# Loading v in f32, updating the state in two operations, and transposing more pairs by the DMA crossbar in a tuned recurrence-plus-MLP kernel

## The chip, the cores and the metric

The kernel runs on one core of one Trainium2 chip. The metric is the device time of one execution in microseconds (us). Each comparison ran on one chip, with runs of the kernel before in between. Every profiled run is of the fast state. Medians are of all runs of a kernel. Ratios leave out the runs classed slow (over 1.5% above the fastest of the same kernel): two of four in the run with a later order, one each in three others, and three of six in one, where it is said.

## The reference

A gated linear recurrence over 768 steps, for 4 batches and 8 heads of 48, feeds an MLP with gelu (384 to 2048 to 384). All inputs and the output are f32.

```python
state = zeros(B, H, D, D)                       # B, H, S, D = 4, 8, 768, 48
for t in range(S):
    state = alpha[:, :, t, :, None] * state + einsum('bhd,bhe->bhde', k[:, :, t], v[:, :, t])
    y[:, :, t] = einsum('bhd,bhde->bhe', q[:, :, t], state)
x = y.transpose(0, 2, 1, 3).reshape(B * S, H * D)
h = x @ w_in                                    # 384 x 2048
out = gelu_tanh(h) @ w_out                      # 2048 x 384
```

## The kernel before

The 768 steps are cut into 6 chunks of 128 tokens, and the 4 batches go in twos: 12 *pairs* (chunk, two batches), numbered 0 to 11. Pair by pair the kernel does this:

- loads a (alpha), q, k, v of the pair from DRAM; GpSimd (POOL) issues these loads for pairs 2 to 11;
- forms the decays (`la` = ln a, a running sum `cum` on TensorE, exps `b`, `binv`, `bend`) on ScalarE (ACT), and the scaled q' (`qp`) and k' (`kp`) on VectorE (DVE);
- transposes q' and k' into `qkT`, multiplies them (`at`), masks the product (`atm`), and forms y (`yps`) from it, v and the state;
- transposes x = y into `xT`, runs layer 1 (`hT`), gelu (`gT`), layer 2 (`acc`), and stores (`ot`).

A transpose is done either by TensorE (a product with an identity matrix, then an eviction from PSUM) or by a DMA through the crossbar, issued by SyncE (SP). Two tuples say which pairs take the DMA. `DECAYS` says in which phase of layer 1 the ln and exps of a pair are done.

```python
DECAYS = {-1: (0, 1), 1: (2, 3), 2: (4,), 3: (5,), 4: (6, 7), 5: (8,), 6: (9,), 7: (10,), 8: (11,)}
TURN_QK, TURN_X = (8, 9, 10, 11), (7, 8, 9, 10, 11)
...
def load(self, n, c, i, lo=0, hi=2):            # n: "a", "q", "k" or "v"
    def emit(e):
        if n not in u:
            u[n] = self.tile(n, [C, 2, H, D], BF16 if n == "v" else F32)
        src = self.src[n][2 * i + lo:2 * i + hi].rearrange("b h s d -> s (b h) d")[c * C:(c + 1) * C]
        (nc.sync if e == "SP" else nc.gpsimd).dma_start(u[n][:, lo:hi].rearrange("t b h d -> t (b h) d"), src)
...
def turn_dma(self, u, n):                       # q' or k' of a pair, both batches
    self.nc.sync.dma_start_transpose(self.qkT(u)[:, "qk".index(n)].rearrange("d i p t -> d (i p) t"),
                                     u[n + "p"].rearrange("t i h d -> t (i h d)"))
def turn_x_dma(self, u, i, c, b):               # x of one batch
    self.nc.sync.dma_start_transpose(self.xT[c][:, :, b, :], u["x", i])
...
def carry(self, u, i, c, b):                    # state update of one batch
    for o in range(2):                          # the two heads of a head pair
        ps, fs = slice(64 * o, 64 * o + 64), slice(D * o, D * o + D)
        acc = kv[ps, :, fs]
        if c > 0:
            nc.vector.tensor_tensor(s[ps], acc, old[ps, :, fs], op=ALU.add)
            acc = s[ps]
        nc.vector.tensor_tensor(new[ps, :, fs], acc, u["bend"][ps, i, :, None].to_broadcast([64, H // 2, D]), op=ALU.mult)
```

Every engine runs its instructions in a fixed order. The program makes it when it is built, by list scheduling over tasks with assumed costs, buffers and landing times. For a transpose by DMA it assumes that the data is there `landed + xbar` after the issue: 2.2 + 1.5 = 3.7 us for q' or k', one after the other, and 3.2 us for x, with 2.5 us more for early pairs (`late`). Where the assumption is too short, an engine stands at an instruction although later ones could run.

```python
landed=2200, xbar_qk=1500, xbar_x=1000, late_x=2500
...
if t.kind in ("turn", "store"):
    xbar = t.done = max(xbar, t.end + W["landed"] - t.xbar) + t.xbar
    t.done += t.late
...
tq = [s.add("turn", {"SP": W["turn"]}, P + 10, self.turn_dma(u, n), d, xbar=W["xbar_qk"])
      for n, d in (("q", qp), ("k", kp))]
```

## Time and profile before

| | before |
|---|---|
| median time | 185.78 us (184.66 to 186.07) |
| span of the profiled run | 183.2 us |
| TensorE busy | 175.7 us, clock granted in full |
| first layer-1 matmul (`hT`) | 17.21 us |

The expectations below say 17.4 us for the first `hT`, as the chain that ended last has its first piece of `hT` at 17.38 us; all starts in this text are from the order on TensorE. TensorE is the bound, as the lines in the prediction show. Two more views also belong here. The first is the table of DMA queues on the page: queue, packets, megabytes, and the time that its packets took as a share of 16 engines. q0 carries the loads that GpSimd issues, q1 what SP issues.

```profile
DMA packets 51206, 27.76 MB, mean 151 GB/s; under 512 B 38833, under 2 KB 48241, under 8 KB 51185
...
q0 software_dynamic: 32096, 17.70, 69.0%
q1 hardware_dynamic: 18512, 9.38, 21.5%
```

Most packets are small. Sorted by size, the trace has 24,576 packets of 96 B (one row of v, cast to bf16 by its load), 2,944 of about 4 KB (f32 loads: 18 to 24 rows of 192 B in a packet, mostly 22) and 12,032 of 256 B (transposes). These counts were there to be read before the prediction, and the prediction does not use them.

The second view is the order on VectorE in the start (start, length, what; in brackets the idle time before it and what ended it):

```profile
11.11 2.48 DVE L431 TENSOR_TENSOR atm<-at,ut 128x512 bf16<-128x512 f32 x4 [0.82 <-PE at L424]
15.38 1.02 DVE L354 TENSOR_TENSOR qp<-q,b 128x384 bf16<-128x384 f32 x2 [1.78 <-ACT x L480]
```

The four masks of pair 0 come first, then the q' of pair 1.

### The profile page before, as it was taken

Reading aid. Unit: us, or ns where it says so; the run is one execution under the profiler, and the core shown is the slowest. Engines: PE = TensorE matmul, PEld = TensorE weight load, DVE = VectorE, ACT = ScalarE, POOL = GpSimd, SP = SyncE. Lnnn points to the kernel's source line nnn. Section 1 sums busy time; section 2 is a strip of 40 time slices with the busy share of each in tenths; the row PEclk is TensorE's granted clock in tenths of the full one; section 3 lists DMA queues with packets and bytes.
Section 4 is the critical chain, followed back from the end, with each engine's and each line's share of the span. In section 5 each row is a group of like instructions: output and inputs, shape, how many; then the busy total and the mean of one; then the engine's idle time right before and its main releaser. Section 6 shows DMA issues by size and latency. Waiting matters only on the chain.

```text
span 183.2 us, 4630 instructions
## 1 busy us (share of the span) xinstructions
PE 175.7 (96%) x1861; PEld 129.3 (71%) x1861; DVE 104.2 (57%) x232; ACT 135.6 (74%) x310; POOL 60.9 (33%) x68
## 2 busy tenths in 40 slices
PE   7887999999999999999999999999999999999993
PEld 2465869666686787687688769678677677686873
DVE  7775954065969896597499798298644715000000
ACT  3666969873888789859799768899789884491941
POOL 2595837975545755564750200000000000000000
PEclk9999999999999999999999999999999999999999
DMA  5999999999999999999999955753271290311102
GB/s 155 187 242 211 187 231 214 204 202 174 195 281 183 169 229 197 181 225 205 180 213 235 179 171 100 104 115 67 52 170 46 43 202 4 88 43 47 43 0 86
DMA packets 51206, 27.76 MB, mean 151 GB/s; under 512 B 38833, under 2 KB 48241, under 8 KB 51185
## 3 DMA queue, kind: packets, MB, share of 16 engines
q0 software_dynamic: 32096, 17.70, 69.0%
q1 hardware_dynamic: 18512, 9.38, 21.5%
q10 hardware_dynamic: 576, 0.39, 0.7%
q8 instruction: 14, 0.23, 0.6%
q14 instruction: 8, 0.06, 0.1%
HBM read 25.17 MB, written 4.72 MB: 163 GB/s over the span
## 4 chain that ended last, share of the span: by engine, by line
PE 85%; DMA 6%; ACT 3%; DVE 2%; SPq 1%; ACTq 1%; issue 0%
PE acc L516 34%; PE hT L497 31%; PE at L424 4%; PE qkT_ps L364 4%; PE yps L473 3%; DMA a<-in_alpha_dram 2%; PE yps L470 2%; DMA q<-in_q_dram 2%; PE cum L320 2%; PE kv L441 2%; DMA qkT<-kp 2%; PE xT_ps L487 1%; DVE atm L431 1%; ACT L503 1%; PE cum L322 1%; SPq L247 1%
## 5 line engine op out<-in xcount | busy, mean ns | idle before, releaser
L497 PE MATMUL hT<-xT,w_in 128*128 128x256 bf16 x576 | 70.1, 273 | 0.4 <-ACT gT L503 0.4
L503 ACT ACTIVATE gT<-hT 128x256 bf16<-128x256 f32 x192 | 63.4, 387 | 8.6 <-PE hT L497 8.3
L516 PE MATMUL acc<-w_out,gT 128*128 128x384 bf16 (+1 forms) x400 | 68.8, 319 | 0.0
L497 PEld LDWEIGHTS <-w_in 128*128 128x128 bf16 x576 | 54.0, 98 | 8.0 <-issue 0.6
L516 PEld LDWEIGHTS <-gT 128*128 128x128 bf16 x400 | 36.8, 98 | 19.6
L431 DVE TENSOR_TENSOR atm<-at,ut 128x512 bf16<-128x512 f32 x48 | 30.9, 685 | 15.0 <-PE at L424 14.5
L354 DVE TENSOR_TENSOR qp<-q,b 128x768 bf16<-128x768 f32 (+1 forms) x15 | 11.7, 794 | 18.7 <-ACT b L343 15.8
L528 ACT COPY ot<-acc 128x384 f32<-128x384 f32 (+1 forms) x18 | 8.3, 462 | 13.9 <-PE acc L516 12.6
L235 POOL DMA_DIRECT2D v<-in_v_dram x13 | 14.6, 1123 | 9.6 <-PE hT L497 2.9
L235 POOL DMA_DIRECT2D k<-in_k_dram x11 | 12.2, 1112 | 11.0 <-DVE kp L354 5.2
L343 ACT ACTIVATE b<-cum 128x768 bf16<-128x768 f32 (+1 forms) x15 | 10.2, 684 | 6.7 <-PE cum L322 3.1
L235 POOL DMA_DIRECT2D q<-in_q_dram x11 | 12.3, 1114 | 7.0 <-DMA k<-in_k_dram 1.8
L235 POOL DMA_DIRECT2D a<-in_alpha_dram x11 | 12.3, 1114 | 5.9 <-ACT gT L503 2.2
L213 ACT ACT_TABLE_LOAD x9 | 11.5, 1283 | 2.8 <-issue 2.6
L480 ACT CAST x<-yps 128x384 bf16<-128x384 f32 x16 | 7.7, 481 | 7.8 <-PE yps L473 7.6
L458 DVE TENSOR_TENSOR st<-stmp,bend 64x192 bf16<-64x192 f32 x32 | 11.3, 353 | 1.5
L354 DVE TENSOR_TENSOR kp<-k,binv 128x768 bf16<-128x768 f32 (+1 forms) x15 | 11.8, 792 | 0.2
L456 DVE TENSOR_TENSOR stmp<-kv,st 64x192 f32<-64x192 f32 x32 | 11.3, 352 | 1.0 <-PE kv L441 0.7
L503 ACT ACT_TABLE_LOAD x9 | 11.5, 1283 | 0.2
L222 PE MATMUL idle<-zero 128*128 128x512 bf16 x27 | 9.5, 462 | 1.2 <-DVE blk L778 1.2
L382 DVE COPY qkT<-qkT_ps 128x1024 bf16<-128x1024 bf16 (+1 forms) x13 | 8.7, 688 | 3.0 <-PE qkT_ps L364 2.9
L343 ACT ACTIVATE binv<-cum 128x768 bf16<-128x768 f32 (+1 forms) x15 | 10.1, 683 | 0.0
(62 smaller groups left out, 159.4 us busy)
## 6 DMA issues: line engine op xcount, KB each, us to landing
out_dram<-ot SPq DMA_DIRECT2D x23, 192.0 KB, 2.3
a<-in_alpha_dram POOLq DMA_DIRECT2D x9, 384.0 KB, 13.1
q<-in_q_dram POOLq DMA_DIRECT2D x9, 384.0 KB, 13.2
k<-in_k_dram POOLq DMA_DIRECT2D x9, 384.0 KB, 13.3
v<-in_v_dram POOLq DMA_DIRECT2D x11, 192.0 KB, 13.3
w_in<-in_moe_w_in_dram POOLq DMA_DIRECT2D x4, 384.0 KB, 7.7
w_out<-in_moe_w_out_dram POOLq DMA_DIRECT2D x4, 384.0 KB, 9.8
a<-in_alpha_dram SPq DMA_DIRECT2D x6, 96.0 KB, 3.4
```

The lines of the kernel that those rows point to most:

```text
L213: nc.scalar.add_instruction(mybir.InstLoadActFuncSet(name=nc.get_next_instruction_name(), act_func_set_id=i, engine=mybir.EngineType.Activ ...
L222: self.nc.tensor.matmul(ps, self.zero[:, 0:self.C], self.zero, start=True, stop=True)
L235: (nc.sync if e == "SP" else nc.gpsimd).dma_start(u[n][:, lo:hi].rearrange("t b h d -> t (b h) d"), src)
L343: self.nc.scalar.activation(u[n].rearrange("t i h d -> t i (h d)")[:, lo:hi], cum, AF.Exp, scale=1.0 if n == "b" else -1.0)
L354: self.nc.vector.tensor_tensor(out, rows, b, op=ALU.mult)
L382: self.copy(e)(t, ps)
L431: self.nc.vector.tensor_tensor(u["atm", i][:, o], u["at", i][o], self.ut[:, None, :].to_broadcast([self.C, self.H // 2, self.C]), op=ALU.mult)
L456: nc.vector.tensor_tensor(s[ps], acc, old[ps, :, fs], op=ALU.add)
L458: nc.vector.tensor_tensor(new[ps, :, fs], acc, u["bend"][ps, i, :, None].to_broadcast([64, H // 2, D]), op=ALU.mult)
L497: self.nc.tensor.matmul(h, self.w_in[:, j, nt * self.C:(nt + 1) * self.C], self.xT[c][:, j, lo:hi].rearrange("p g t -> p (g t)"), start=j ...
L503: return lambda e: self.nc.scalar.activation(self.gT[c % self.NG][:, nt, lo * self.C:hi * self.C], f.pop(("h", c, lo, nt)), AF.Gelu_apprx_ ...
L516: self.nc.tensor.matmul(f["acc", c, b][:, lo:hi], self.gT[c % self.NG][:, nt, b * self.C:(b + 1) * self.C], self.w_out[:, nt, lo:hi], star ...
```

## The change

Four things change together; letters are used below.

- **A**: v arrives in f32 by plain loads and is narrowed to bf16 on chip, by VectorE for pairs 0 and 1 and by GpSimd for the others.
- **B**: the state update covers both heads of a head pair in one add and one multiply of 128x384, with decays `ends` that are zero off the diagonal blocks.
- **C**: q', k' of pairs 5, 6, 7 and x of pairs 5 and 6 are transposed by DMA as well, so that TensorE does less.
- **D**: the decays of pair 5 move to the phase of pair 4's, and pair 6's one phase ahead.

```diff
-    DECAYS = {-1: (0, 1), 1: (2, 3), 2: (4,), 3: (5,), 4: (6, 7), 5: (8,), 6: (9,), 7: (10,), 8: (11,)}
+    DECAYS = {-1: (0, 1), 1: (2, 3), 2: (4, 5), 3: (6,), 4: (7,), 5: (8,), 6: (9,), 7: (10,), 8: (11,)}
-    TURN_QK, TURN_X = (8, 9, 10, 11), (7, 8, 9, 10, 11)
+    TURN_QK, TURN_X = (5, 6, 7, 8, 9, 10, 11), (5, 6, 7, 8, 9, 10, 11)
-    BUFS = dict(..., ot=6, bend=8, a=4, q=4, k=4, v=6)
+    BUFS = dict(..., ot=5, bend=3, ends=8, a=4, q=4, k=4, v=3, vb=4)
...
-                u[n] = self.tile(n, [C, 2, H, D], BF16 if n == "v" else F32)
+                u[n] = self.tile(n, [C, 2, H, D], F32)
+    def narrow(self, u, lo, hi):
+        (self.nc.gpsimd.tensor_copy if e == "POOL" else self.nc.vector.tensor_copy)(u["vb"][...], u["v"][...])
+    def ends(self, u):
+        nc.vector.tensor_tensor(ends, bend broadcast, self.half broadcast, op=ALU.mult)     # 16 elements
...
-            for o in range(2):
-                ... two operations of 64x192 each
+            nc.vector.tensor_tensor(s, acc, old, op=ALU.add)
+            nc.vector.tensor_tensor(new..., acc..., ends, op=ALU.mult)
```

The diff is shortened; `...` marks what is left out. The assumed costs of v's loads in the start (`early_0`, `early_1`, `share`) and of the state operations change with it. The assumed landing of a transpose does not.

More of the change, by code (lines that the diff above doesn't have):

```diff
@@ L17 @@
     cum=530, cum_packed=1500, t8=450, t4=225, attn=340, kv=170, inter=170, intra=205, tx=168, l1_4=655, l1_2=340, l2=655,
-    qk2=910, qk1=500, ev8=650, ev4=350, mask=640, st=1400, st0=700, xc=520, xe=330, ot=540,
+    qk2=910, qk1=500, ev8=650, ev4=350, mask=640, st=1090, st0=545, end=110, xc=520, xe=330, ot=540,
     ev8_act=960, ev4_act=520, xc_act=450, xe_act=450, ot_act=450,
-    strip=2120, cast=1500, weight=2080, dma=2100, issue=1100, wissue=760, sp=100, store=2600, turn=1250, landed=2200, xbar_qk=1500, xbar_x=1000, late_x=2500, piece=330, late_k=1500, piece_issue=450, begin=2700, cast_0=1300, share=1200, cast_1=1900, ln_packed=1040, cold=380, fill=216, zero=1100,
+    strip=2120, weight=2080, dma=2100, issue=1100, wissue=760, sp=100, store=2600, turn=1250, landed=2200, xbar_qk=1500, xbar_x=1000, late_x=2500, piece=330, late_k=1500, piece_issue=450, begin=2700, early_0=1000, share=1000, early_1=1400, vb1=300, vb2=550, vb1_pool=600, vb2_pool=950, ln_packed=1040, cold=380, fill=216, zero=1100,
 )
@@ L156 @@
     URGENT = (2,)
-    BUFS = dict(ca=1, yk=2, ff=4, la=3, qp=4, kp=4, b8=2, kn=2, qkT=4, atm=6, x=3, ot=6, bend=8,
-                a=4, q=4, k=4, v=6)
+    BUFS = dict(ca=1, yk=2, ff=4, la=3, qp=4, kp=4, b8=2, kn=2, qkT=4, atm=6, x=3, ot=5, bend=3, ends=8,
+                a=4, q=4, k=4, v=3, vb=4)
     def __init__(self, ctx, tc, q, k, v, alpha, w_in, w_out, out):
@@ L182, in __init__ @@
         self.ident = const.tile([C, C], BF16, name="ident")
+        self.half = const.tile([C, 2], F32, name="half")
         self.ones = const.tile([C, 1], F16, name="ones")
@@ L345, in exp, with emit @@
         return emit
+    def narrow(self, u, lo, hi):
+        def emit(e):
+            if "vb" not in u:
+                u["vb"] = self.tile("vb", [self.C, 2, self.H, self.D], BF16)
+            (self.nc.gpsimd.tensor_copy if e == "POOL" else self.nc.vector.tensor_copy)(u["vb"][:, lo:hi].rearrange("t b h d -> t (b h d)"), u["v"][:, lo:hi].rearrange("t b h d -> t (b h d)"))
+        return emit
     def scaled(self, u, n, lo, hi):
@@ L441, in emit @@
                 nc.tensor.matmul(kv[:, p, :], u["kn" if u["packed"] else "kp"][:, i, 2 * p:2 * p + 2, :].rearrange("t h d -> t (h d)"),
-                                 u["v"][:, i, 2 * p:2 * p + 2, :].rearrange("t h d -> t (h d)"),
+                                 u["vb"][:, i, 2 * p:2 * p + 2, :].rearrange("t h d -> t (h d)"),
                                  start=True, stop=True)
+        return emit
+    def ends(self, u):
+        C, H = self.C, self.H
+        def emit(e):
+            t = u["ends"] = self.tile("ends", [C, 2, H // 2, 2], F32)
+            (self.nc.gpsimd if e == "POOL" else self.nc.vector).tensor_tensor(
+                t.rearrange("f i p o -> f (i p) o"), u["bend"].rearrange("f i p -> f (i p)")[:, :, None].to_broadcast([C, H, 2]),
+                self.half[:, None, :].to_broadcast([C, H, 2]), op=ALU.mult)
         return emit
@@ L449, in emit @@
         def emit(e):
-            kv, old, new = u["kv", i], self.state[b][c % 2], self.state[b][(c + 1) % 2]
-            for o in range(2):
-                ps, fs = slice(64 * o, 64 * o + 64), slice(D * o, D * o + D)
-                acc = kv[ps, :, fs]
-                if c > 0:
-                    s = self.sb.tile([C, H // 2, D], F32, tag=f"stmp{o}", bufs=2, name="stmp")
-                    nc.vector.tensor_tensor(s[ps], acc, old[ps, :, fs], op=ALU.add)
-                    acc = s[ps]
-                nc.vector.tensor_tensor(new[ps, :, fs], acc,
-                                        u["bend"][ps, i, :, None].to_broadcast([64, H // 2, D]), op=ALU.mult)
+            acc, old, new = u["kv", i], self.state[b][c % 2], self.state[b][(c + 1) % 2]
+            if c > 0:
+                s = self.sb.tile([C, H // 2, 2 * D], F32, tag="stmp", bufs=2, name="stmp")
+                nc.vector.tensor_tensor(s, acc, old, op=ALU.add)
+                acc = s
+            ends = u["ends"][:, i].rearrange("f p o -> f (p o)")[:, :, None].to_broadcast([C, H, D])
+            nc.vector.tensor_tensor(new.rearrange("f p (o d) -> f (p o) d", o=2),
+                                    acc.rearrange("f p (o d) -> f (p o) d", o=2), ends, op=ALU.mult)
         return emit
@@ L472, in emit @@
             for h in range(H):
-                nc.tensor.matmul(y[:, h, :], u["atm", i][:, h % 2, h // 2, :], u["v"][:, i, h, :],
+                nc.tensor.matmul(y[:, h, :], u["atm", i][:, h % 2, h // 2, :], u["vb"][:, i, h, :],
                                  start=c == 0, stop=True, skip_group_check=True)
@@ L548, in load @@
             nonlocal n
-            land = W[{"v": "cast", "w": "weight"}.get(key[0], "strip")]
-            loads[key] = s.add("load", {"POOL": cost}, n, emit, gate, land=W[f"cast_{key[1]}"] if key[0] == "v" and key[1] in self.PACKED else land * 3 // 8 if key[0] != "w" and key[1] in self.SPLIT else land,
+            land = W[{"w": "weight"}.get(key[0], "strip")]
+            loads[key] = s.add("load", {"POOL": cost}, n, emit, gate, land=W[f"early_{key[1]}"] if key[0] == "v" and key[1] in self.PACKED else land * 3 // 8 if key[0] != "w" and key[1] in self.SPLIT else land,
                                late=W["share"] if key[:2] == ("v", 0) else 0)
@@ L599, in tasks @@
             early = m in self.EARLY
-            lns[m], ends[m], qp, kp, be = [], [], [None, None], [None, None], [None, None]
+            lns[m], ends[m], qp, kp, be = [], [], [None, None], [None, None], []
             cums, exps = [], []
@@ L611, in tasks @@
                 if u["sums"]:
-                    be[lo:hi] = [x[2]] * n
+                    be.append(x[2])
                 ends[m].append(x[-1])
@@ L644, in tasks @@
                 owner = every[0]
+            if u["sums"]:
+                end = s.add("end", {"DVE": W["end"]}, P + 16, self.ends(u), be)
+            narrow = [None, None]
+            for lo, hi in ((0, 1), (1, 2)) if early else self.parts(m):
+                n = hi - lo
+                narrow[lo:hi] = [s.add("vb", {"DVE": W[f"vb{n}"]} if early else {"POOL": W[f"vb{n}_pool"]}, P + 9 if early else -1, self.narrow(u, lo, hi),
+                                       [loads["v", m, lo]])] * n
+            loads["v", m, 0].take("v", *narrow)
             for j in range(2):
@@ L670, in tasks @@
                 y = s.add("y", {"PE": W["intra"] + (W["inter"] if c else 0)}, P + 20 + j, self.y(u, j, c, b),
-                          ms + turned + [loads["v", m, j]] + ([states[b, c - 1]] if c else []))
+                          ms + turned + [narrow[j]] + ([states[b, c - 1]] if c else []))
                 xc = s.add("x", {"ACT": W["xc_act"], "DVE": W["xc"]}, P + 20 + j, self.x(u, j), [y])
@@ L692, in tasks @@
                         backs.append(tb)
-                    kv = s.add("kv", {"PE": W["kv"]}, P + 30 + j, self.kv(u, j), [k, loads["v", m, j]])
+                    kv = s.add("kv", {"PE": W["kv"]}, P + 30 + j, self.kv(u, j), [k, narrow[j]])
                     st = states[b, c] = s.add("st", {"DVE": W["st" if c else "st0"]}, P + 30 + j, self.carry(u, j, c, b),
-                                              [kv, be[j]] + ([states[b, c - 1], ys[b, c - 1]] if c else []))
+                                              [kv, end] + ([states[b, c - 1], ys[b, c - 1]] if c else []))
                     kv.take("yk", st)
@@ L710, in tasks @@
             kp[0].take("kp", *tq, *kvs)
-            loads["v", m, 0].take("v", *vs)
+            narrow[0].take("vb", *vs)
             if u["sums"]:
-                be[0].take("bend", *cs)
+                be[0].take("bend", end)
+                end.take("ends", *cs)
         n = 0
@@ L778, in run @@
         nc.vector.memset(self.blk, 0.0)
+        nc.vector.memset(self.half, 0.0)
+        for o in range(2):
+            nc.vector.memset(self.half[64 * o:64 * o + 64, o:o + 1], 1.0)
         for t in self.ut_blk:
```

## The prediction

> **What bounds the kernel now.** I read the busy table and the slices first. TensorE (PE) is busy 96% of the span and its clock is granted in full in every slice, so PE is the candidate; a mean hides stages, so I asked for the busy time by stretch next.
>
> ```profile
> PE 175.7 (96%) x1861; PEld 129.3 (71%) x1861; DVE 104.2 (57%) x232; ACT 135.6 (74%) x310; POOL 60.9 (33%) x68
> ...
> PE   7887999999999999999999999999999999999993
> ...
> DMA  5999999999999999999999955753271290311102
> ```
>
> ```profile
> 17.00:28.50 11.50, 11.24 (x142) 8.84 (x140) 8.00 (x17) 9.10 (x24) 7.59 (x10) 1.00 1.46 206
> 28.50:180.30 151.80, 151.20 (x1601) 113.01 (x1598) 84.28 (x165) 117.14 (x266) 43.59 (x39) 1.00 0.88 144
> ```
>
> The second fence has two stretches: length, then busy PE, weight loads, DVE, ACT, POOL. From 28.5 to 180.3 us PE idles 151.80 - 151.20 = 0.6 us. Before that lie a start bounded by loads and by short DVE and ACT steps, and after it a tail of 2.9 us of eviction and store. "Busy" could be padding, so I checked the pace in the chain that ended last: 48 matmuls of hT in 5.24 us are 109 ns each, and 16 of acc in 2.60 us are 163 ns each, without holes. So the middle is a full PE pipe: a matmul taken away there is time taken away, as long as nothing new makes PE wait. The other row that matters is DMA: full until slice 23 (some 107 us) and mostly idle afterwards.
>
> These lines of the chain (start, length, what) are the PE work that the change moves off PE:
>
> ```profile
> 77.44 0.89 PE qkT_ps L364 x16
> ...
> 86.67 0.17 PE xT_ps L487 x3
> ...
> 91.80 0.89 PE qkT_ps L364 x16
> ```
>
> Sixteen transposes turn q' and k' of one pair of batches, in 0.89 us (55.6 ns each); three turn x of one batch, in 0.17 us.
>
> [...] The trace has 352 and 353 ns for the two state operations and 552 to 555 ns for 128x384 products[...]. [...] an output store, also issued by SP, takes 7.7 us to land beside the loads and 2.1 us after them. [...]
>
> **The change, part by part.**
>
> *Transposes by DMA for more pairs.* q' and k' of pairs 5, 6, 7 leave PE: 3 x 16 x 55.6 ns = 2.67 us. x of pairs 5 and 6 leaves PE: 2 pairs x 2 batches x 3 x 55.6 ns = 0.67 us. All of it lies in the stretch from 77 to 107 us, where PE never idles: **3.34 us off the path**. The evictions go from DVE too: 6 of qkT at 687 ns and 4 of xT at 352 ns, 5.5 us, beside PE work and worth nothing by themselves. In their place come 6 transposes of q', k' and 4 of x on the SP queue. What they take when the queue is quiet, and what the load beside them does, is here (first row from 30 to 108 us, the others from 108 to 160 us; the last number is us from issue to landing):
>
> ```profile
> out_dram<-ot SPq DMA_DIRECT2D x11, 192.0 KB, 7.7
> ```
>
> ```profile
> out_dram<-ot SPq DMA_DIRECT2D x9, 192.0 KB, 2.1
> xT<-x SPq DMA_TRANSPOSE x10, 2.3
> qkT<-qp SPq DMA_TRANSPOSE x4, 3.2
> qkT<-kp SPq DMA_TRANSPOSE x4, 3.1
> ```
>
> All eight transposes of q', k' and all ten of x now run after the loads. The new ones run among them. If they lose what a store loses (7.7 - 2.1 = 5.6 us), q' and k' land some 9 us after issue and x some 8 us: an estimate from these rows.
>
> *Decays one phase ahead.* This is to pay for that latency. Pair 5's ln and exps move from ACT's turn at 71 to 77 us to the one at 56 to 64 us, beside pair 4's; pair 6's from the turn at 85 to that at 71. The count of turns stays nine, so table loads stay 18 x 1.28 us. A turn with two pairs is longer: the present one runs 85.27 to 94.05 us, 8.8 us, against 71.12 to 77.41, 6.3 us, for one pair. PE lost nothing at the present double turn (10.00 of 10.00 us busy from 80 to 90 and from 90 to 100), since it has 5.2 us of acc and the pair's attention to do; the new double turn also still has pair 4's transposes on PE. So I count 0. Inputs: a of pair 5 was issued at 42.55 us and lands some 13.1 us later, at 55.7; its q and k at about 58 and 59.4, just in time for products at 61 to 64.
>
> Timing for pair 5: transposes issued at about 64 to 66 us, landed at 67 to 69 (quiet) or 73 to 75 (loaded). The present at of pair 5 starts at 78.99, so data that late still meets the present position. x: even if its y stays at 82.5 and 85.5 us, x is issued by about 86.5 and lands by 94.5 loaded, against hT of pair 5 at about 91.8; but attention that is ready earlier is placed earlier, as with pairs 8 to 11 now, and then x has over 8 us.
>
> *v in f32.* [...] POOL issues at the pace of landings from 55 to 95 us;[...] steps are 1.5 to 1.9 us for a v load and 1.7 to 2.2 us for an f32 one. Some 0.35 us more for ten loads is 3.5 us of DMA time, all before 108 us and off the path. Narrowing on POOL: nine of 128x768 and two halves[...]. On DVE: four narrowings of 128x384 for pairs 0 and 1, at most 0.56 us each, in the start. No transpose now runs while a casting load is in flight (the last v lands at about 99 us, the first transpose is at 110.04), and I take it that v goes to f32 to let transposes in earlier.
>
> *State update.* Now:
>
> ```profile
> L458 DVE TENSOR_TENSOR st<-stmp,bend 64x192 bf16<-64x192 f32 x32 | 11.3, 353 | 1.5
> L456 DVE TENSOR_TENSOR stmp<-kv,st 64x192 f32<-64x192 f32 x32 | 11.3, 352 | 1.0 <-PE kv L441 0.7
> ...
> L458 DVE TENSOR_TENSOR st<-kv,bend 64x192 bf16<-64x192 f32 x8 | 2.8, 355 | 0.8 <-ACT gT L503 0.7
> ```
>
> 25.4 us in all. [...] DVE is 57% busy and PE waits for it only in the start, so I count 0 in the middle.
>
> **The sum.** 3.34 us off PE. In the start, narrowing v of pairs 0 and 1 on DVE can put 0.2 to 0.5 us ahead of the first hT, and the shorter first state updates give back some; I count a loss of 0.3 us. 185.8 - 3.3 + 0.3 = **182.8 us**, 1.6% less.
>
> **The rivals.** (a) *A new wait of PE for a transpose under load.* For: PE executes in a fixed order made with an assumed landing of 3.7 us for q', k' (2.2 + 1.5 in the kernel's own table) and nothing for load, where stores lose 5.6 us; if at is placed as soon as the order thinks it ready, PE stands for the difference. x has 2.5 us of allowance. Against: at also waits for one shared PSUM buffer, and hT can run first. One stall of 2 to 5 us would give 185 to 188 us; small ones 183 to 184. (b) *DMA or POOL becomes the bound:* POOL waits for v to land before it can narrow, holds back later loads, and ACT's new double turn starts late for want of a, q, k of pair 5, which have 1 to 2 us in hand. It would give 183.5 to 185. Against: about six loads stand in the queue, 13 us of work. (c) *More than PE's share:* the start is gated by DVE steps of 0.3 to 0.7 us and contains fills of PE; if f32 v lands sooner and DVE is freer, 0.5 to 1.5 us more, 181 to 182. (d) *ACT becomes the bound* as PE's phases shorten to about 12.5 us: against it, the present phase without PE transposes, 128.40 to 140.78 us, shows PE full and ACT below 80%.
>
> **Range and chances.** The gain of PE work is nearly certain, its keeping is not. Half of (c) gives 181, a moderate (a) or (b) 185.5: range 181.0 to 185.5. Faster by over 2% means below 182.06, which needs about 0.4 us of (c) beyond the pure PE gain: 0.31. Slower by over 2% needs stalls of 7 us in all: 0.05. Within 2%: 0.64.
>
> **What would show it.** PE transposes fall by 48 and 12, to 80 of q', k' (of 128) and 30 of x (of 42). In the middle PE idles under 1 us; if (a) holds, waits of PE or its weight loads for DMA qkT or DMA xT appear at 65 to 108 us. [...] The first hT stays within 0.5 us of 17.2 us. DMA stays full some 4 to 8 us longer. The prediction is wrong if transposes under load take over 10 us, or if the start moves by over 1 us.

## The result, and the profile after

| | before, same rounds | after |
|---|---|---|
| median time | 185.22 us (184.31 to 186.07) | 224.12 us (223.19 to 224.63) |
| ratio | | 1.209 (95%: 1.202 to 1.217) |
| span of the profiled run | 183.2 us | 222.2 us |
| TensorE busy | 175.7 us | 180.0 us |

Ratios here are the mean time of one kernel's fast runs over the mean of the other's fast runs of the same rounds, so they are not quite the ratio of the medians. The kernel is 21% slower, far outside the range.

The busy table and the slices of the kernel after (40 slices of 5.6 us; PE and DMA in tenths busy, PEclk the granted clock in tenths):

```profile
PE 180.0 (81%) x1804; PEld 129.4 (58%) x1804; DVE 100.4 (45%) x209; ACT 134.0 (60%) x304; POOL 69.3 (31%) x79
...
PE   7859999999999104991089806989999999999993
...
PEclk9999999999999755999559975899999999999999
DMA  5999999999999995199913993160341706130102
```

TensorE has three deep holes, and after each its clock is at about half (a 5 in the slices above). The waits say at what it stands (engine, line, what ended the wait: total us, times, longest):

```profile
PEld L432 <- DMA qkT<-kp: 34.5, 5, 13.7
PE at L432 <- DMA qkT<-kp: 33.2, 4, 13.4
POOL a L236 <- ACT x L496: 17.8, 2, 17.3
...
POOL vb L352 <- PE yps L489: 14.6, 1, 14.6
```

The chain that ended last holds the same three transposes, of pairs 5, 6 and 7 (start, length, what), 44 us in all:

```profile
19.57 0.49 PE hT L513 x3
...
68.73 17.54 DMA qkT<-kp
...
97.32 14.60 DMA qkT<-kp
...
123.49 11.83 DMA qkT<-kp
```

The landings, from the view of DMA issues cut at 60, 80, 110 and 140 us, one pair in each (the last number is us from issue to landing; the same transposes took 3.2 and 3.1 us before):

```profile
qkT<-qp SPq DMA_TRANSPOSE x1, 18.7
qkT<-kp SPq DMA_TRANSPOSE x1, 17.5
...
qkT<-qp SPq DMA_TRANSPOSE x1, 6.6
qkT<-kp SPq DMA_TRANSPOSE x1, 14.6
...
qkT<-qp SPq DMA_TRANSPOSE x1, 10.9
qkT<-kp SPq DMA_TRANSPOSE x1, 11.8
```

**Where the 39.0 us went.** TensorE's idle time grew from 183.2 - 175.7 = 7.5 us to 222.2 - 180.0 = 42.2 us, that is by 34.7 us; 33.2 us of it is the wait of `at` for k'. Its busy time grew by 4.3 us although 60 transposes left it. The work removed was 3.3 us, so the rest runs 7.6 us longer. Some 1.0 us of that is three more padding matmuls; the remaining 6.6 us fits the half clock after the holes (for example 0.50 granted from 86 to 88 us, 0.72 from 88 to 90, 1.00 from 90 on). The trace's record of the clock has it at half until 89.1, 116.4 and 140.3 us, that is over 2.8, 4.5 and 4.9 us of work after the three holes; half of these 12.2 us is 6.1 us. The holes are of 13.4, 11.0 and 8.5 us, and the record has half clock from 75.45, 106.17 and 130.07 us, that is from 2.6, 5.2 and 3.2 us into them. Shorter holes in the experiments below went both ways. One of 2.3 us (43.3 to 45.6 us) in the first run of "One pair less" was followed by half clock from 46.6 to 53.5 us, and three of 0.7 to 0.94 us between 92.3 and 95.8 us in the run with small packets on the kernel before by half clock from 95.2 to 98.6 us. One of 2.9 us in the run with small packets and a later order was not. What length of hole brings the half clock is not shown by these runs.

**Why the transposes were late.** The records of the DMA packets were counted by queue and size. Rates are packets per us of each of the 16 engines:

| stretch | f32 load packets (4 KB, about 290 ns each) | transpose packets (256 B, about 30 ns each beside loads, 18 ns without) |
|---|---|---|
| after, 74 to 78 us | 3.2 | 3.7 |
| after, 78 to 82 us | 3.2 | 4.8 |
| after, 82 to 86.5 us | 1.2 | 19.3 |
| after, 172 to 180 us, no loads | 0 | 19.0 |

The first row can be read, near enough, from the view of DMA queues for 74 to 78 us (queue: packets of all 16 engines, megabytes, share; 34 of the packets of q0 are not of a load but of 4 B):

```profile
q0 software_dynamic: 237, 0.83, 94.0%
q1 hardware_dynamic: 236, 0.06, 11.4%
```

While both queues have work, one transpose packet goes through for about each load packet: 3.7 and 4.8 beside 3.2 in the first two rows. I read this as each engine taking the two queues in turn, a packet from each. That is my estimate from the near equality of the two columns; the order in which an engine takes packets was not looked at. A load packet of 290 ns and a transpose packet of 30 ns, one after the other, would let about 3.1 of each through per us. Where few loads are queued, the counts part: from 98 to 102 us, POOL having just issued again, 19.4 transpose packets passed beside 1.9 load packets.

q' of a pair is 1,024 packets, and k' another 1,024: 128 per engine. At 3.7 per us they need 35 us. They did not need that long because the stall itself ended it: with TensorE at `at`, buffers were not freed, POOL stood (17.8 and 14.6 us above, and 17.3 us more in a line left out), no new loads were issued, the queue ran dry between 82 and 84 us and the transposes then went at 19 per us.

### The profile page after: what moved, and what is told of

Its sections match the earlier page's. It is cut to its first block, busy times and chain, and to the rows that moved or that the text cites. A ratio compares the mean times of both kernels' runs of the same rounds, so it can differ in the third digit from the quotient of the medians.

```text
span 222.2 us, 4524 instructions
## 1 busy us (share of the span) xinstructions
PE 180.0 (81%) x1804; PEld 129.4 (58%) x1804; DVE 100.4 (45%) x209; ACT 134.0 (60%) x304; POOL 69.3 (31%) x79
## 4 chain that ended last, share of the span: by engine, by line
PE 62%; DMA 25%; DVE 3%; ACT 3%; issue 2%; SPq 2%; POOL 0%; DVEq 0%; ACTq 0%
PE acc L532 26%; PE hT L513 22%; DMA qkT<-kp 21%; PE at L432 3%; DMA q<-in_q_dram 3%; PE yps L489 2%; SPq L248 2%; PE yps L486 2%; PE qkT_ps L372 1%; PE cum L321 1%; DMA a<-in_alpha_dram 1%; ACT L519 1%; PE xT_ps L503 1%; PE idle L223 1%; PE kv L449 1%
## 5 line engine op out<-in xcount | busy, mean ns | idle before, releaser
L519 ACT ACTIVATE gT<-hT 128x256 bf16<-128x256 f32 x192 | 64.1, 386 | 45.7 <-PE hT L513 45.1
L513 PE MATMUL hT<-xT,w_in 128*128 128x256 bf16 x576 | 72.8, 281 | 1.1 <-ACT gT L519 1.1
L513 PEld LDWEIGHTS <-w_in 128*128 128x128 bf16 x576 | 56.0, 100 | 11.1 <-issue 2.5
L432 PE MATMUL at<-qkT 64*128 64x128 bf16 x192 | 10.2, 233 | 33.2 <-DMA qkT<-kp 33.2
L432 PEld LDWEIGHTS <-qkT 64*128 64x128 bf16 x192 | 5.9, 99 | 39.2 <-DMA qkT<-kp 34.5
L236 POOL DMA_DIRECT2D a<-in_alpha_dram x11 | 12.2, 1108 | 38.1 <-ACT x L496 17.8
L362 DVE TENSOR_TENSOR qp<-q,b 128x768 bf16<-128x768 f32 (+1 forms) x15 | 11.8, 793 | 14.3 <-ACT b L344 11.9
L236 POOL DMA_DIRECT2D q<-in_q_dram x11 | 12.2, 1106 | 6.5 <-DVE qp L362 3.3
L236 POOL DMA_DIRECT2D k<-in_k_dram x11 | 12.2, 1107 | 3.5 <-DMA w_out<-in_moe_w_out_dram 1.2
L352 POOL CAST vb<-v 128x768 bf16<-128x768 f32 (+1 forms) x11 | 8.5, 783 | 14.6 <-PE yps L489 14.6
L362 DVE TENSOR_TENSOR kp<-k,binv 128x768 bf16<-128x768 f32 (+1 forms) x15 | 11.8, 792 | 0.1
L223 PE MATMUL idle<-zero 128*128 128x512 bf16 x30 | 10.5, 454 | 1.2 <-DVE half L804 1.2
L474 DVE TENSOR_TENSOR st<-stmp,ends 128x384 bf16<-128x384 f32 x16 | 10.6, 664 | 0.5
L496 ACT CAST x<-yps 128x384 bf16<-128x384 f32 x11 | 5.3, 478 | 8.1 <-PE yps L489 7.7
## 6 DMA issues: line engine op xcount, KB each, us to landing
a<-in_alpha_dram POOLq DMA_DIRECT2D x9, 384.0 KB, 12.2
q<-in_q_dram POOLq DMA_DIRECT2D x9, 384.0 KB, 12.5
```

Of the source, the lines that this page charges most:

```text
L223: self.nc.tensor.matmul(ps, self.zero[:, 0:self.C], self.zero, start=True, stop=True)
L352: (self.nc.gpsimd.tensor_copy if e == "POOL" else self.nc.vector.tensor_copy)(u["vb"][:, lo:hi].rearrange("t b h d -> t (b h d)"), u["v"][ ...
L362: self.nc.vector.tensor_tensor(out, rows, b, op=ALU.mult)
L432: nc.tensor.matmul(at[o][:, p, :], t[sl, 1, p, :], t[sl, 0, p, :], start=True, stop=True)
L474: nc.vector.tensor_tensor(new.rearrange("f p (o d) -> f (p o) d", o=2), acc.rearrange("f p (o d) -> f (p o) d", o=2), ends, op=ALU.mult)
L513: self.nc.tensor.matmul(h, self.w_in[:, j, nt * self.C:(nt + 1) * self.C], self.xT[c][:, j, lo:hi].rearrange("p g t -> p (g t)"), start=j ...
```

## The experiments

Fourteen kernels were run; all gave correct results. Twelve came before and two after the last open question was stated.

### Undo C alone

```diff
-    TURN_QK, TURN_X = (5, 6, 7, 8, 9, 10, 11), (5, 6, 7, 8, 9, 10, 11)
+    TURN_QK, TURN_X = (8, 9, 10, 11), (7, 8, 9, 10, 11)       # from the kernel after
```

> The changed kernel with q', k' of pairs 5 to 7 and x of pairs 5, 6 turned on TensorE again; f32 v, narrowing, two-operation state and earlier decays stay. Theory (T): the loss is TensorE standing before the late q', k' transposes, 33 us of waits and some 5 us of slow clock after them; without them 185 to 189 us, and no wait of TensorE over 2 us after 30 us. Rival (R1): f32 v, the narrowing on POOL or the earlier decays hold up the inputs and the transposes are only where it shows; then above 200 us.

Measured: 188.26 us against 185.68, ratio 1.017 (1.010 to 1.025). Nothing waits for `qkT`, and TensorE waits 2.2 us at most for any one thing. So C with its waits is some 36 of the 39 us; A, B and D keep a loss of some 2.6 us. The loss is in the start: the first `hT` is at 20.91 us instead of 17.21. DMA is full only to slice 19 of 40 here, against slice 23 before, so loading v in f32 did not lengthen that stretch; that it shortened it is not shown, since with B alone and v still cast (below) DMA is full to slice 18.

### C and D alone, on the kernel before

```diff
-    DECAYS ... 2: (4,), 3: (5,), 4: (6, 7) ...     # from the kernel before
+    DECAYS ... 2: (4, 5), 3: (6,), 4: (7,) ...
-    TURN_QK, TURN_X = (8, 9, 10, 11), (7, 8, 9, 10, 11)
+    TURN_QK, TURN_X = (5, 6, 7, 8, 9, 10, 11), (5, 6, 7, 8, 9, 10, 11)
```

> The kernel before with only the transposes and the earlier decays of the change; v cast by the DMA, four-operation state. T: loads stand in the queue as before, so the waits of at for qkT come here too: 205 to 230 us. R1, or that plain f32 v loads are what delays the transposes (R3): under 195 us.

Measured: 223.44 us, ratio 1.210 (1.198 to 1.222). The wait:

```profile
PE at L424 <- DMA qkT<-kp: 36.4, 4, 20.8
```

The stall is there in full with v cast by its load and the old state update. A and B neither cause it nor cure it. The first `hT` is at 17.36 us, so C and D do not move the start. Part of this stall is of another kind than the one worked out above; see what stays open.

### Tell the order that q', k' land late

```diff
-  self.turn_dma(u, n), d, xbar=W["xbar_qk"])
+  self.turn_dma(u, n), d, xbar=W["xbar_qk"], late=14000 * (m < 8))   # from the kernel after
```

> The changed kernel, with 14 us added to the landing that the order assumes for q', k' of pairs 0 to 7, so that TensorE gets at of these pairs later. T: the transposes still take over 10 us to land beside the loads, but TensorE has other work in front of them: waits for qkT fall from 33 us to under 6, 184 to 191 us. If the transposes cost more than a badly placed wait (they hold up the loads, R4), above 200 us.

Measured: 221.53 us, ratio 1.186 (1.170 to 1.201); the expectation was missed. TensorE went on past the old place, so loads went on too, and q', k' of pair 5 took longer than before:

```profile
qkT<-qp SPq DMA_TRANSPOSE x1, 26.0
qkT<-kp SPq DMA_TRANSPOSE x1, 30.6
...
PE at L432 <- DMA qkT<-kp: 13.6, 2, 12.4
...
PE hT L513 <- DMA xT<-x: 8.7, 1, 8.7
```

The number came out where the expectation had put its rival. From 74 to 91 us, 3.0 load packets and 3.5 transpose packets passed per us and engine: the shares of the kernel after, for 17 us on end. From 91 to 101 us the loads thinned out as well (1.6 per us), so the 30.6 us stay somewhat under the 35 us worked out above. This separates two readings: it was not only an order that knew too little, the transposes lacked throughput beside the loads. A phase takes some 12.5 us, and in it q', k' and the x of two batches need 128 + 48 packets per engine, which at 3 to 4 per us is over 40 us.

### Smaller load packets

```diff
-                u[n] = self.tile(n, [C, 2, H, D], F32)      # from the kernel after
+                u[n] = self.tile(n, [C, 2, H, D], F32 if u["m"] < 3 else F16 if n == "a" else BF16)
```

The loads of pairs 3 to 11 cast, so they move in packets of 96 B, one row each. It rounds the inputs earlier and is not meant as a version to keep.

> The changed kernel, with a (to f16), q, k and v (to bf16) of pairs 3 to 11 cast by the DMA: the same number of 192-byte rows, but I expect one small packet per row instead of packets of 4 KB. T in the form that transposes share the DMA engines packet by packet with the loads (T-packet): q', k' of pairs 5 to 7 land in 3 to 7 us and the time is 182 to 190 us. Rival (R2): the DMA engines are full and a transpose waits for its share of bytes or behind what is queued, whatever the packets: 11 to 19 us to land, over 205 us. The result may be off by more than the reference allows, since a, q, k are rounded earlier.

Measured: 207.27 us, ratio 1.120 (1.110 to 1.130). q' and k' land in 7.3 to 9.0 us. From 71 to 75 us, where both queues have work throughout, the view of DMA queues has:

```profile
q1 hardware_dynamic: 1736, 0.44, 83.4%
q0 software_dynamic: 1854, 0.18, 80.9%
```

That is 27 and 29 packets per us and engine: about one for one again, with some nine times as many load packets as above (29 against 3.2), each of 28 ns instead of 290. The packet size is the cause, then: the order is the same and the bytes read are the same. (The edit also halves the bytes that these loads write. The DMA engines were full in these 4 us all the same; a run with fewer bytes in packets of 4 KB was not made.) The landing stays above the assumed 3.7 us, so TensorE still stands:

```profile
PE at L432 <- DMA qkT<-kp: 16.2, 4, 6.1
```

### Smaller packets and an order that knows

```diff
+  late=7000 * (m < 8)                              # on top of the run with smaller load packets
```

> The run with a, q, k, v cast by the DMA from pair 3 on (one 96-byte packet per row), with 7 us added to the landing that the order assumes for q', k' up to pair 7. Theory: with small packets in the other queue the crossbar has the throughput, 7 to 9 us a pair, so once the order knows it TensorE need not stand: waits for qkT fall from 16 us to under 4, 184 to 190 us. Rival: with the loads going on (they no longer stop in a stall) the transposes slow down again, as in the run with plain loads and a later order: over 198 us.

Measured: 189.72 us, ratio 1.020 (1.010 to 1.031). The wait is almost gone, with landings of 7.0 us (median) and 10.0 us (longest):

```profile
PE at L432 <- DMA qkT<-kp: 3.2, 2, 2.9
```

34 of the 39 us are recovered by the two together: share of the engines, and an order that knows what is left. What remains: the first `hT` is 2.0 us late (19.25 us), and TensorE idles 4.5 us from 100 to 120 us, at k' (2.9 us) and at x (1.6 us); against that, its busy time is 173.7 us, 2.0 us less than before.

### The start: v of pairs 0 and 1

```diff
-                u[n] = self.tile(n, [C, 2, H, D], F32)      # from the run that undid C
+                u[n] = self.tile(n, [C, 2, H, D], BF16 if n == "v" and u["packed"] else F32)
```

The copy on VectorE stays, bf16 to bf16.

> The run with the transposes back on TensorE, in which v of pairs 0 and 1 is cast by the DMA again (a bf16 to bf16 copy on DVE stays in the place of the narrowing, so only the DMA changes). That run lost 2.6 us against before, and its trace has a of pair 1 landing 1.5 us later and the first hT 3.5 us later. Theory: the plain f32 load of v moves in 4 KB packets, and the small loads of a and q beside it get a packet in between each; with the cast one-row packets are back: first hT at 17 to 18.5 us, 184.5 to 186.3 us. Rival: the DVE operations added in the start (narrowing, masked decays) are the cause: still 187.5 to 189 us.

Measured: 187.30 us, ratio 1.012 (1.006 to 1.018); missed, for I expected the start back. `la` of pair 1 is at 11.49 us, as before, but the first `hT` is at 20.02. The order on VectorE shows why:

```profile
15.28 0.56 DVE L362 TENSOR_TENSOR qp<-q,b 128x384 bf16<-128x384 f32 x1 [2.02 <-DMA q<-in_q_dram]
15.75 2.48 DVE L439 TENSOR_TENSOR atm<-at,ut 128x512 bf16<-128x512 f32 x4
```

VectorE stands 2.02 us for a q of pair 1 and only then masks pair 0, 4.6 us later than before (11.11). The changed tasks and assumed costs of the start had put q' ahead of the masks, and on a fixed order a late load then holds work that was ready. A later run (under "One pair less") drops these copies, and the masks come back to 11.26 us.

### The state update alone

On the kernel before, B only: the two-operation `carry`, `ends`, and their buffers.

> The kernel before with only the two-operation state update (and its smaller bend and ot buffers). The theory says the state update is not on the path in the middle, since PE idles 0.6 us there; and that the start loss of the changed kernel comes from v in f32 and its narrowing, not from the state. Then: 184.5 to 186 us, ratio 0.995 to 1.005, first hT within 0.5 us of 17.4 us, state operations near 664 ns with the decays, DVE busy some 3 us lower. The rival, that the changed priorities of the state operations alone reorder DVE in the start, would show a first hT at 19 us or later and 187 us.

Measured: 185.61 us against 184.96, ratio 1.003 (0.999 to 1.007); first `hT` at 17.04 us. B makes no difference that these runs resolve, and it does not disturb the start; nor do C and D (17.36 us above). What is left for the start's loss is A, with the narrowing on VectorE and the order that comes of it. My 664 ns in that expectation was a misreading: the multiply took 558 ns here on average and the add 549 ns, near the 552 to 555 ns of the 128x384 products in the trace before. The 664 ns was a mean in the kernel after that a few long ones had raised, see below.

### x alone

```diff
-    TURN_QK, TURN_X = (5, 6, 7, 8, 9, 10, 11), (5, 6, 7, 8, 9, 10, 11)   # from the kernel after
+    TURN_QK, TURN_X = (8, 9, 10, 11), (5, 6, 7, 8, 9, 10, 11)
```

> The changed kernel with q', k' of pairs 5 to 7 back on TensorE, but x of pairs 5 and 6 still by the crossbar: 24 packets on each DMA engine for one x, against 128 for q' and k' of a pair. Packet theory: 24 packets at 3 to 4 per us beside the loads are 6 to 8 us, two behind each other 10 to 15 us, of which most is covered before hT: 187 to 195 us, waits of hT for xT under 8 us in all. Rival (a transpose waits until the loads in the queue have drained, whatever its size): x takes 12 us or more each and the time is over 200 us.

Measured: 189.75 us, ratio 1.022 (1.013 to 1.030), with the first `hT` at 22.09 us in the profile. x landed in 6.1 us at most and nothing waited for it. An x of one batch is 384 packets, 24 per engine. I took from this that x is harmless. The same on the kernel before said otherwise:

```diff
-    TURN_QK, TURN_X = (8, 9, 10, 11), (7, 8, 9, 10, 11)                  # from the kernel before
+    TURN_QK, TURN_X = (8, 9, 10, 11), (5, 6, 7, 8, 9, 10, 11)
```

> The kernel before with one change: x of pairs 5 and 6 also by the DMA crossbar, q' and k' as before from pair 8, decays as before. The theory says that the 24 packets per engine of an x get through beside the loads within the slack that x has: landings of x under 8 us, no wait of PE for xT above 0.5 us, PE's transposes of x 12 fewer (0.67 us): 184.0 to 185.2 us, ratio 0.993 to 1.000. The rival, that transposes beside loads cost whatever their size, says a wait for xT of over 2 us and 187 us or more.

Measured: 195.02 us, ratio 1.054 (1.049 to 1.059); missed. The two x of pair 5 landed after 12.2 and 13.4 us:

```profile
PE hT L497 <- DMA xT<-x: 6.4, 1, 6.4
```

### One pair less: two attempts at a faster version

First the change without the narrowing in the start, and with q', k' by DMA from pair 7 and x from pair 6 (v of pairs 0 and 1 cast straight into its place, 3 us more of assumed landing for pair 7):

> A version meant to keep what is good: two-operation state, f32 v narrowed on POOL from pair 2 on, v of pairs 0 and 1 cast by the DMA straight to bf16 (no narrowing), earlier decays, q', k' by the crossbar from pair 7 and x from pair 6 on, when the queue of loads has thinned out. Against the run with the transposes on TensorE: less 3.5 us of start, less 0.89 us (q', k' of pair 7) and 0.33 us (x of pair 6): 183.5 to 185.5 us. If pair 7 still meets the loads: a wait for qkT of over 3 us and 187 to 195 us.

Measured: 189.63 us, ratio 1.024 (1.016 to 1.032); missed. No transpose was waited for (landings of q' and k' up to 5.2 us), but another part of A was:

```profile
PE yps L491 <- POOL vb L354: 2.9, 2, 2.3
```

GpSimd issues the loads and narrows v, in one fixed order, so TensorE waits for a narrowing that stands behind load issues. Half clock followed, 0.66 from 46 to 48 us and 0.50 from 48 to 52 us. What was won is the start: the first `hT` is at 16.94 us. With v of pairs 0 and 1 cast by its load and no copy on VectorE, the masks of pair 0 run at 11.26 us, before the q' of pair 1. So the start's loss is with the copies of v for pairs 0 and 1 on VectorE and the assumed costs that go with them.

Then the kernel before with D, q', k' from pair 7 (4 us more of assumed landing) and x from pair 5:

> The kernel before with decays as in the change, q' and k' by DMA from pair 7 on (4 us more of assumed landing for pair 7) and x from pair 5 on; v stays cast by DMA, the state stays in four operations. The theory (a transpose beside loads moves few of its 256-byte packets; pair 7's run when the loads are nearly through; x has few packets) says: landings of q', k' under 8 us, no wait of PE for qkT above 1 us, the start as before (first hT within 0.5 us of 17.4 us), 1.6 us fewer of PE: 183.5 to 185 us. The rival, that any transpose beside loads costs more than it saves, says 186.5 us or more.

Measured: 201.85 us, ratio 1.069 (1.063 to 1.075), missed. The six runs fall in two groups, 196.5 to 198.9 us and 204.8 to 206.1 us; the second is classed slow, and the ratio and the profile are of the first.

```profile
PE at L424 <- DMA qkT<-kp: 9.9, 1, 9.9
```

One pair beside the loads costs a stall of about 10 us, a quarter to a third of what three cost.

### All of C and D with small packets, on the kernel before

As in the run with smaller packets and an order that knows, but v by the old load and the old state update.

> The kernel before with decays one phase ahead and q', k', x of pairs 5 to 11 by DMA as in the change; v cast by DMA, the state in four operations; a, q, k of pairs 3 to 11 cast by their loads as well (96-byte packets), and 7 us more of assumed landing for q', k' of pairs 5 to 7. The theory says that small load packets let a transpose through in 7 to 10 us, that the order knows it, and that the start is as before: 183 to 185 us, PE transposes 3.3 us fewer, waits for qkT under 3 us in sum. The rival, that the 256-byte packets of a transpose lose as much to any load, says landings over 15 us and over 195 us.

Measured: 189.89 us, ratio 1.026 (1.023 to 1.030). q' and k' landed in 6.9 to 7.9 us (medians of those beside loads), and the waits for them fell to 2.0 us, as expected; the time did not reach 185. The start is as before (`hT` at 17.46 us), and TensorE now loses its time in many small pieces: 2.5 us idle from 80 to 100 us with the clock at 0.91, 1.2 us from 100 to 120, 1.7 us from there to 180. The clock was at half from 95.2 to 98.6 us, after three holes of 0.94 us at most. So with the landing repaired and known to the order, and the start untouched, the 3.3 us of TensorE's work were still not won.

### Does a casting load of v make the difference?

Still open was why x landed in at most 6.1 us in one kernel (v in f32) and in 12 to 13 us in the other (v cast). The two runs on the kernel before with x from pair 5, and with q', k' from pair 7, were repeated with v of pairs 3 to 11 in f32, narrowed by GpSimd (and with the change's buffers for v and `ot`).

> The run with x alone from pair 5 on the kernel before (195.0 us, landings of x 12 to 13 us, PE stalled 6.4 us), with v of pairs 3 to 11 loaded in f32 and narrowed by GpSimd. If casting loads of v slow a transpose beside them: x lands in 4 to 7 us, no wait of PE for xT above 0.5 us, first hT near 17.4 us, 184 to 185.5 us. If it was the place in time alone: landings of x of 10 us or more again, and 190 us or more.

Measured: 193.35 us, ratio 1.044 (1.040 to 1.049). x of pairs 5 and 6 landed in 5.9 to 8.6 us and nothing waited for it, but the pipeline had slipped beforehand by a wait for a narrowing, so those transposes met other loads:

```profile
PE kv L451 <- POOL vb L354: 4.2, 1, 4.2
```

> The run with q', k' from pair 7 and x from pair 5 (201.9 us, k' of pair 7 landing after 15.5 us, PE stalled 9.9 us), with v of pairs 3 to 11 in f32 and narrowed by GpSimd. If casting loads of v slow a transpose beside them: q', k' of pair 7 land in 5 to 9 us, PE waits under 2 us for them, 183.5 to 187 us. If packets of 4 KB do the same harm: landings of 10 us or more, 193 us or more.

Measured: 207.27 us, ratio 1.116 (1.111 to 1.121). Here x landed in 15.2 to 22.1 us:

```profile
PE hT L507 <- DMA xT<-x: 10.4, 1, 10.4
```

From 92 to 100 us, 2.8 to 3.1 transpose packets passed per us and engine beside 2.4 to 2.8 load packets of 4 KB; the x of two batches is 48 packets, 48 / 2.8 = 17 us. So the type of v does not decide. What goes with a late x is how many loads are queued in that moment, to judge by how long the loads issued from 82 to 104 us took to land themselves (medians of each of a, q, k, v):

| run | v | loads landed after, us | x landed after, us |
|---|---|---|---|
| x alone, from the kernel after | f32 | 5.4 to 6.4 | 6.1 at most |
| x alone, on the kernel before, v in f32 | f32 | 8.7 to 10.5 | 5.9 to 8.6 |
| x alone, on the kernel before | cast | 13.6 to 14.9 | 12.2 to 13.4 |
| q', k' from pair 7, v in f32 | f32 | 14.4 to 15.4 | 15.2 to 22.1 |

No run changed the number of queued loads alone.

No version beat the kernel before.

## Why the prediction was wrong

**The step that failed** is the estimate of a transpose under load: "If they lose what a store loses (7.7 - 2.1 = 5.6 us), q' and k' land some 9 us after issue". It carried a delay over as a constant per transfer. A constant part there is: beside loads the first packet of pair 5 moved 5.0 us after the issue (66.81 to 71.83 us), against 1.3 us in a quiet queue (110.04 to 111.31 us in the kernel before). The rest I put down to the count of packets. A store of 192 KB is 128 packets of 1,536 B, 8 per engine; q' or k' of a pair is 64 per engine. If one packet goes through for each load packet (an estimate from the 3.7 to 4.8 beside 3.2 per us above), eight times the packets wait eight times as often. Measured: 17.5 and 18.7 us for pair 5 with the loads dying out, 26.0 and 30.6 us when they went on, against the 9 us of the prediction. It had named "over 10 us" as a sign of being wrong.

**Rival (a) was the right mechanism at the wrong size.** It named the fixed order, the assumed 3.7 us and the wait at `at`; it sized it at "2 to 5 us", once. Measured: four waits of 33.2 us in sum, three of them long (holes of 13.4, 11.0 and 8.5 us). A term was missing beside it, the half clock after a hole, some 6.6 us. The argument against it, that hT can run first, fails on a fixed order: what stands ahead stands ahead.

**Pair 5's timing.** Even by the prediction's own 9 us the data would have met the "present position" of `at`, but the order moved `at` forward to where 3.7 us allowed it, and TensorE stood there from about 73 us instead of using the data at 78.99. The prediction named this in its rival and for other pairs and did not apply it here. It also dated the inputs by median landings (13.1 us for a), where the trace before has 14.5 us for pair 5's a and q and 15.2 us for its k; the transposes were issued at 66.8 and 68.7 us, not at 64 to 66. That is small beside the rest.

**The purpose given to A.** "I take it that v goes to f32 to let transposes in earlier": no run supports it. The stall is the same with cast v (223.44 and 224.12 us), and the pair of runs meant to show it failed to.

**DMA time of v in f32** was predicted as 3.5 us more, with DMA full 4 to 8 us longer. No run shows that: DMA is full to slice 19 instead of 23 when only C was undone. With B alone and v still cast it is full to slice 18, so the shorter stretch cannot be put down to v's type either.

**The start** was put at +0.3 us. It was +2.4 us in the kernel after (first `hT` 19.57 us), up to 3.7 us with C undone; "over 1 us" was the other sign of being wrong that the prediction had named. The terms counted were durations of narrowings; the cost came through the order on VectorE.

**What held.** The gain on TensorE's work, in counts: transposes by TensorE fell to 80 of q', k' and 30 of x. The groups by form of the kernel after (count | total, mean ns):

```profile
L474 DVE TENSOR_TENSOR st<-stmp,ends 128x384 bf16<-128x384 f32 x16 | 10.6, 664 | 0.5
L471 DVE TENSOR_TENSOR stmp<-kv,st 128x384 f32<-128x384 f32 x16 | 8.8, 549 | 0.8 <-PE kv L449 0.8
L352 POOL CAST vb<-v 128x768 bf16<-128x768 f32 x9 | 7.5, 841 | 14.6 <-PE yps L489 14.6
```

The add is at 549 ns, beside 552 to 555 ns for the 128x384 products in the trace before, and the narrowing of 128x768 on GpSimd is at 0.84 us. The multiply is at 664 ns in the mean, but ten of its 16 took 0.56 us; the longest took 1.21 us (at 70.17) and 1.12 us (at 92.23). Narrowings on GpSimd alone do not explain them: in the run that undid C, with the same narrowings, the mean is 561 ns, and with B alone, without them, 558 ns. Why these few are long stays open. The mean of `ends` is 167 ns with B alone and 231 ns in the kernel after. All of it lies beside TensorE's work.

**What stays open.** In some stretches both queues are slow at once: from 102 to 110 us in the kernel after, load packets of 4 KB took 513 to 539 ns in the mean, and only about 0.9 of them and 4 to 9 transpose packets passed per us and engine. In the run with x alone on the kernel before, 96-B packets took 192 to 298 ns from 88 to 92 us, six to ten times their usual 30. In the run with C and D alone the stall at pair 5 has such a stretch too: from 78 to 81 us 96-B packets took 362 ns, and 1.1 transpose packets passed per us. One transpose packet for each load packet does not explain this. The landings of 14.6 and 11.8 us of pairs 6 and 7 lie in or near such stretches, so the count of packets accounts for pair 5 of the kernel after and for the run with a later order, and only in part for the other stalls. With small load packets all these landings shortened to 10.0 us at most, and from 66 us on no stretch of 4 us had a mean of over 53 ns for 96-B packets. The start's loss is placed with the copies of v for pairs 0 and 1; whether the copies or their assumed costs reorder VectorE was not taken apart.

## What to carry to other kernels

Before a DMA is put beside others, count its packets and theirs, not bytes alone: per us and engine, 3.7 to 4.8 transpose packets of 256 B passed here beside 3.2 load packets of 4 KB, some 27 beside 29 of 96 B, and 19.0 without loads. At one for each load packet, 64 packets at 3.2 per us take 20 us (an estimate; q' and k' of pair 5 took 18.7 and 17.5 us with the loads dying out, and 3.2 and 3.1 us without loads). On a fixed order the assumed landing has to be the loaded one, and where the throughput is short a longer assumption did not help (221.53 us with 14 us more), because TensorE stalled less at k' (13.6 us instead of 33.2) and the competing loads kept coming (3.0 packets per us and engine from 74 to 91 us). A saving of 3.3 us on the bound engine was not worth a dependence on a queue that is full at that time; the place for these transposes is after the loads, where the kernel before had them.
